# A state-space scan with a gated MLP: the rounding word of the weights is added on GpSimd from the fourth piece on

## The chip, the core and the metric

The kernel runs on one core of a Trainium2 chip. The metric is the device time of one execution in microseconds (us). The inputs lie in HBM, the output is written there.

## What is computed

Two stages. The first is a scan with decays, in chunks, over 4 batches x 8 heads x 768 tokens (head size 32, state size 16); the second is a gated MLP over the 3072 tokens of 256 channels, with 1536 hidden channels.

```python
la = log_a[:, :, sl]
cum = np.cumsum(la, axis=-1)
L = np.exp(cum[:, :, :, None] - cum[:, :, None, :]) * causal
M = np.einsum('bhin,bhjn->bhij', Cc, Bc) * L
y[:, :, sl] = np.einsum('bhij,bhjd->bhid', M, xc) + y_inter
...
state = decay_full[:, :, None, None] * state + np.sum(Bx, axis=2)
...
x = attn_out.transpose(0, 2, 1, 3).reshape(B * S, H * D)
g = x @ w_gate
silu = g * (1.0 / (1.0 + np.exp(-g)))
out = (silu * (x @ w_val)) @ w_out
```

The three weight matrices come as 64-bit floats. The kernel makes 32-bit floats of them itself.

## The kernel before

**Tiling.** The 768 tokens are cut into 6 blocks k of 128; a block with its 4 batches is a tile of 512 columns. Each block goes through the scan (tiles L, E, bc, xb, Cz, S, st, T, y), then through the MLP's gate and value products gv for the 12 pieces f of the hidden channels, the product sg of gate and value, the split of sg into a high part hh and a low part hl, and the projection po, whose result is drained to ob and stored. The last two blocks are multiplied as a pair with fewer products (px, py, pz, pr).

**Weights.** There are 18 pieces: wg0 to wg11 for gate and value, wo0 to wo5 for the projection. A piece i is fetched as 128 x 512 pairs of 32-bit words (tile wg3r, say: the low words `lw` are every second word, the high words `hw` the others). ScalarE makes the magnitude from the high word (`w_magnitude`, tile wg3w), VectorE bounds it (`w_range`), ScalarE makes the sign and exponent part (`w_sign`) and either engine the rest of the low word, scaled to one word (`w_rest`). VectorE shifts and joins them (`w_shift`, SCALAR_TENSOR_TENSOR in the trace), and `w_round` adds the rest as an integer. In the trace of before that addition is the row CUSTOM_DVE_ANT_0, in the order listings it is ISA. Block 0 multiplies pieces 0 to 8 with these 32-bit floats directly (gv<-xf,wg3w); pieces 9 to 11, the projection's pieces and all later blocks use a high part (wg3h, `w_high`) and a low part (wg3l, `w_low`).

**Buffers.** A raw piece lies in one of eight places until it is rounded; the fetch of a later piece into the same place waits for that (`uses=[("raw", i)]` in the plan). The fetches stand in SP's queue with the loads of bc, xb, L and E.

**What sets the order.** A planner (`Plan`) knows every step with its engine, its cost on that engine, its rank and the steps that it needs. It fills each engine's queue in turn, and what it finds is issued as it stands; each engine then works through its queue in that order. A step that may run on two engines goes where the planner's times favour it, so a changed cost or engine of one step moves others too. The rank of the rounding and what it needs stand in line 865:

```python
add("DVE", 0.6, do(w_round, i), r - 3.3 if i else -0.94,
    [("shift", i), ("rest", i), *([] if i else [("ce", 0)])], uses=[("raw", i)], gives=("round", i))
```

In the listings below sg_3_474<-gv_3_1_470 is the product of piece 3 (470 and 474 are buffer numbers), L<-L,dj a scan of the decays, L<-S,L a mix of decays with scores, T a state step.

Of the kernel before, what the change touches and what calls it, by code (L numbers as in the profile page):

```python
# [15 lines left out]
ALU = mybir.AluOpType  # L16
# [27 lines left out]
class Plan:  # L44
# [25 lines left out]
    def add(self, engine, cost, run, rank, needs=(), takes=(), uses=(), gives=None, kind=None, lag=0.0, rows=1.0, slack=0.0):  # L70
        engines = [(engine, cost)] if cost is not None else engine
        self.ops.append(Op(engines, run, rank, needs, takes, uses, gives, kind, lag, rows, slack))
# [137 lines left out]
def scan_moe_kernel(ctx: ExitStack, tc, rows, decays, bc, xb, wgv, wo, cst, out):  # L210
    nc = tc.nc
    PSUM = bass.MemoryType.PSUM
    te, ve, se, ge, sp = (
        Ordered(tc, e) for e in (nc.tensor, nc.vector, nc.scalar, nc.gpsimd, nc.sync)
    )

    def pool(name, bufs, stack=ctx, **kw):
        return stack.enter_context(tc.tile_pool(name=name, bufs=bufs, **kw))
# [5 lines left out]
    raw = pool("raw", RAW)  # L224
# [314 lines left out]
    def raw_home(i):  # L539
        if RAW <= i < RAW + MIXED:  # L540
            return mixed, "ws", "ws"
        if i == RAW + MIXED:
            return mixed, "mix", "mix"
        return raw, "wraw", "raw"
# [5 lines left out]
    part = [dict() for _ in pieces]  # L550
# [40 lines left out]

    def w_round(i):
        w = part[i]["w"]
        ve.tensor_tensor(out=w, in0=w, in1=part[i]["lw"], op=ALU.add)

    def w_high(i, e):
        hi = part[i]["hi"] = wts.tile([P, 4 * P], F32R, name=f"{pieces[i][4]}h")
# [133 lines left out]
    def gate_val(k, f, m):  # L731
        t = hid.setdefault((k, f), {})["gv"[m]] = ps_mm.tile([P, T], F32, tag="mm", name=f"gv{k}_{f}_{m}")
        if not k and f < WHOLE:
            w = part[f]["w"].bitcast(F32).rearrange("p (a b c) -> p a b c", b=2, c=P)
# [57 lines left out]
    rest = {}  # L792
# [20 lines left out]
    def do(f, *a):  # L813
        return lambda *e: f(*a, *e)
# [6 lines left out]
    add = plan.add  # L821
# [3 lines left out]
    for k in range(NB):  # L825
        begin[k] = t
        if k == PAIR:
            begin[k + 1], begin_sum[k], begin_sum[k + 1] = t, t + PAIR_LAG, t + NF * (GVP + PO)
            break
        t += (NF * GV if k else WHOLE * PACE0 + (NF - WHOLE) * GV) + ATT  # L830
        for i in (() if not k else (0, 1) if k == 1 else (k,)):
# [3 lines left out]
    def due(k, f=0):  # L835

        return begin[k] + f * (GV if k else PACE0) - (0 if k else max(f - WHOLE, 0) * (PACE0 - GV))

    def due_sum(k, f):
        return begin_sum[k] + f * (PO if k != PAIR else GVP + PO)  # L840
# [15 lines left out]
    for i in range(NW):  # L856
        r = due(0, i) - 1.0 if i < NF else due_sum(0, 2 * (i - NF)) - 1.0
        add("SP", 0.48, do(w_fetch, i), r - 9.0, [HELD[i]] if i in HELD else [] if not i else [("E", 0)] if i < HASTE else [("asked", 1)], takes=[(raw_home(i)[2], ("raw", i))], gives=("raw", i), lag=1.75 if i >= RAW + MIXED else 3.3 if not i else 1.4)
        plan.marked[plan.ops[-1]] = ("sent", i)
        add("Act", 0.565, do(w_magnitude, i), r - 5.5, [("raw", i)] + ([("xf", 2 * K - 1)] if i else []) + ([("rest", 1)] if i in (2, 3) else []), takes=[("sg" if i < NF else "w", ("w", i))], gives=("mag", i))  # L860
        add("DVE", 0.335, do(w_range, i), r - 4.5 if i else -1.05, [("mag", i)] + ([("round", 0), *([("round", 1)] if i == 2 else [])] if i > 1 else []), gives=("range", i))
        add([("Act", 0.57), ("DVE", 0.335)][: 1 + (i > 2)], None, do(w_rest, i), r - 4.5, [("mag", i), ("sign", i)], gives=("rest", i))
        add("Act", 0.57, do(w_sign, i), r - 5.4, [("mag", i)], gives=("sign", i))
        add("DVE", 0.6, do(w_shift, i), r - 4.2 if i else -1.05, [("range", i), ("sign", i)], gives=("shift", i))
        add("DVE", 0.6, do(w_round, i), r - 3.3 if i else -0.94, [("shift", i), ("rest", i), *([] if i else [("ce", 0)])], uses=[("raw", i)], gives=("round", i))
        early = WHOLE <= i < NF
        if i < NF and not early:
            r = due(1, i) - LATER
        later = [("M", 1, NP - 1)] if i < WHOLE else []
        add([("Act", 0.525), ("DVE", 0.34)], None, do(w_high, i), r - 2.7, [("round", i), *later], gives=("wh", i))  # L870
        whole_done = [("gv", 0, i, m) for m in range(2)] if i < WHOLE else []
        add("DVE", 0.6, do(w_low, i), r - 1.5, [("wh", i), *whole_done], uses=[("w", i)], gives=("wl", i))
# [7 lines left out]
    for k in range(NB):  # L880
        r = due(k)
# [3 lines left out]
        add("-", 0.0, do(new_decays, k) if k else lambda: None, z - 12, [("decays", k - 1)] if k else [], takes=[("L", L), ("E", E)], gives=("decays", k))  # L885
        late = [("raw", LATE[k])] if k in LATE else []

# [13 lines left out]
        if not k:  # L901
# [3 lines left out]
            for b in range(BATCH + 1):  # L905
                for i in range(2 if b < BATCH else 1):
                    t = ("spread", b, i)
                    last_one = int(i and b == BATCH - 1)
                    r = z + (3.0 if b == BATCH else 0.1 * b + i * (0.15 if b == BATCH - 1 else 0.5))
# [37 lines left out]
        uses = [L, E, XB, BC, *y, TT]  # L947
# [36 lines left out]
    r = due(PAIR) - 8.0  # L984
# [18 lines left out]
    for f in range(NF):  # L1003
        r = due(PAIR, f)
        slot = ("raw" if in_raw(f) else "ws", ("ws", f))
        for n, cost in enumerate((0.6, 0.2, 0.335, 0.2)):
            need = [("ws", f, n - 1)] if n else [("wl", f), MIXED_AFTER, *([("ws", f - 1)] if f else [])]
            gives = ("ws", f, n) if n < 3 else ("ws", f)
# [9 lines left out]
        w = [("wl", f), ("wh", f)]  # L1018
# [22 lines left out]
    for k in range(NB):  # L1041
        xs = [(t, k, i) for t in ("xh", "xl") for i in range(2 * K)]
        for f in range(NF):
            r = due(k, f)
# [15 lines left out]
            r = due_sum(k, f) - 4  # L1060
# [4 lines left out]
        for n, (m, t, fs) in enumerate(sums_of(k)):  # L1065
# [4 lines left out]
            r = due_sum(k, fs[0]) + n * 0.01  # L1070
# [22 lines left out]


WHOLE = 9
LATE = {2: NF + 2}
GATE, HASTE = dict(bc=0, aj=0, xb=0, an=1), 7
HELD = {1: ("M", 0, 0), 2: ("M", 0, 1), 3: ("M", 0, 3)}
# [52 lines left out]
```

## Time and profile before

| | |
|---|---|
| Median of 3 runs | 345.58 us |
| Lowest and highest | 344.18 and 346.75 us |
| Span of the profiled execution | 341.9 us |
| Median less that span | 3.7 us |
| TensorE busy | 337.3 us |
| VectorE busy | 256.8 us |
| ScalarE busy | 173.4 us |
| GpSimd busy | 4.1 us |

The profiled execution's own time is its span, from the first to the last instruction; the times of the runs also hold what lies around it. TensorE's matmuls are pipelined and their ends are modelled; start times are what to read there. A busy time counts an instruction from its start to its end; since the next may start a little before, what one costs in a full queue is the time from start to start.

### The profile page before, as it was taken

Reading aid. Unit: us, or ns where it says so; the run is one execution under the profiler, and the core shown is the slowest. Engines: PE = TensorE matmul, PEld = TensorE weight load, DVE = VectorE, ACT = ScalarE, POOL = GpSimd, SP = SyncE. Lnnn points to the kernel's source line nnn. Section 1 sums busy time; section 2 is a strip of 40 time slices with the busy share of each in tenths; the row PEclk is TensorE's granted clock in tenths of the full one; section 3 lists DMA queues with packets and bytes.
Section 4 is the critical chain, followed back from the end, with each engine's and each line's share of the span. In section 5 each row is a group of like instructions: output and inputs, shape, how many; then the busy total and the mean of one; then the engine's idle time right before and its main releaser. Section 6 shows DMA issues by size and latency. Waiting matters only on the chain.

```text
span 341.9 us, 7521 instructions
## 1 busy us (share of the span) xinstructions
PE 337.3 (99%) x3165; PEld 260.7 (76%) x3165; DVE 256.8 (75%) x473; ACT 173.4 (51%) x315; POOL 4.1 (1%) x11
## 2 busy tenths in 40 slices
PE   8999999999999999999999999999999999999996
PEld 7544457888777888877788778877788888888895
DVE  6999999979697586553599943595869999856540
ACT  3696897372684552421344432323656556444542
POOL 1300000000000000000000000000000000000000
PEclk9999999999999999999999999999999999999999
DMA  7789535950000931000380107500010000000101
GB/s 257 259 263 334 176 120 173 220 172 1 0 2 15 254 108 62 0 2 2 124 191 0 63 2 206 105 2 2 3 63 0 0 3 0 0 0 2 51 11 63
DMA packets 10602, 28.29 MB, mean 83 GB/s; under 512 B 1096, under 2 KB 2120, under 8 KB 10568
## 3 DMA queue, kind: packets, MB, share of 16 engines
q1 hardware_dynamic: 10152, 27.57, 27.3%
q8 instruction: 25, 0.41, 0.5%
q10 hardware_dynamic: 416, 0.23, 0.2%
q14 instruction: 9, 0.07, 0.1%
HBM read 24.46 MB, written 3.35 MB: 81 GB/s over the span
## 4 chain that ended last, share of the span: by engine, by line
PE 89%; DMA 5%; ACT 4%; SPq 0%; issue 0%; ACTq 0%
PE gv L199 34%; PE po L199 30%; PE py L199 7%; PE y L199 5%; PE px L199 5%; DMA wg9r<-in_wgv 4%; PE pr L199 2%; PE pz L199 2%; PE S L199 2%; DMA bc<-in_bc 1%; PE st L199 1%; PE rest L199 1%; ACT sg L199 1%; ACT Cz L199 0%; ACT wg9r L199 0%; ACT wg2r L199 0%
## 5 line engine op out<-in xcount | busy, mean ns | idle before, releaser
L199 ACT CAST hh<-sg 128x512 fp32r<-128x512 f32 x70 | 43.4, 621 | 51.2 <-PE po L199 29.0
L199 DVE TENSOR_TENSOR hl<-sg,hh 128x512 fp32r<-128x512 f32 x72 | 49.3, 689 | 25.8 <-ACT hh L199 25.5
L199 ACT ACTIVATE sg<-gv 128x512 f32<-128x512 f32 x48 | 28.5, 595 | 50.6 <-PE gv L199 50.4
L199 DVE TENSOR_TENSOR sg<-gv,sg 128x512 f32<-128x512 f32 x48 | 32.8, 686 | 27.1 <-PE gv L199 27.0
L199 DVE TENSOR_TENSOR_SCAN L<-L,dj 128x520 f32<-128x520 f32 x20 | 23.9, 1227 | 0.0
L199 DVE TENSOR_TENSOR L<-S,L 128x512 f32<-128x512 f32 x24 | 15.0, 683 | 0.4 <-PE S L199 0.4
L199 PE MATMUL py<-xht,ws 128*128 128x512 f32 x48 | 14.8, 389 | 0.0
L199 ACT COPY ob<-po 128x512 f32<-128x512 f32 (+1 forms) x12 | 6.6, 551 | 13.1 <-PE po L199 12.5
L199 ACT ACTIVATE sg<-px 128x512 f32<-128x512 f32 x12 | 7.2, 598 | 10.9 <-PE px L199 10.9
L199 ACT ACTIVATE Cz<-bc,cs 128x512 f32<-128x512 f32 x12 | 8.0, 714 | 8.5 <-DMA bc<-in_bc 8.5
L199 DVE TENSOR_TENSOR mix<-mix 128x128 f32<-128x128 f32 (+1 forms) x36 | 11.9, 330 | 0.2
L199 DVE TENSOR_TENSOR ps<-py,ps 128x512 f32<-128x512 f32 x12 | 8.2, 686 | 4.8 <-PE py L199 4.8
L199 PEld LDWEIGHTS y<-L,xb 64*32 64x32 f32 x768 | 7.3, 105 | 5.0 <-issue 2.8
L199 PE MATMUL y<-L,xb 64*32 64x64 f32 x768 | 10.9, 222 | 0.0
L199 PEld LDWEIGHTS py<-xht,ws 128*128 128x128 f32 x48 | 9.0, 188 | 1.9
L199 PE MATMUL po<-hh,wo0h 128*128 128x512 f32 (+1 forms) x26 | 10.3, 394 | 0.0
L199 PE MATMUL po<-hh,wo2h 128*128 128x512 f32 (+1 forms) x26 | 9.9, 382 | 0.0
L199 PE MATMUL po<-hh,wo3h 128*128 128x512 f32 (+1 forms) x26 | 9.9, 381 | 0.0
L199 PE MATMUL y<-bc,T 32*64 32x64 f32 x352 | 9.9, 228 | 0.0
L199 PE MATMUL po<-hh,wo5h 128*128 128x512 f32 (+1 forms) x26 | 9.8, 378 | 0.0
L199 PE MATMUL po<-hh,wo4h 128*128 128x512 f32 (+1 forms) x26 | 9.8, 378 | 0.0
L199 PE MATMUL po<-hl,wo0h 128*128 128x512 f32 (+1 forms) x26 | 9.7, 375 | 0.0
(485 smaller groups left out, 875.0 us busy)
## 6 DMA issues: line engine op xcount, KB each, us to landing
L<-clipped SPq DMA_DIRECT2D x10, 520.0 KB, 9.7
xb<-in_xb SPq DMA_DIRECT2D x6, 768.0 KB, 5.1
bc<-in_bc SPq DMA_DIRECT2D x6, 512.0 KB, 9.2
out<-ob SPq DMA_DIRECT2D x11, 256.0 KB, 2.1
E<-clipped SPq DMA_DIRECT2D x5, 260.0 KB
wg0r<-in_wgv SPq DMA_DIRECT2D x1, 512.0 KB, 7.4
wg1r<-in_wgv SPq DMA_DIRECT2D x1, 512.0 KB
wg2r<-in_wgv SPq DMA_DIRECT2D x1, 512.0 KB, 4.2
```

The costliest lines, as they stand in the source:

```text
L199: ins = getattr(self.engine, name)(*a, **k)
```

## The change

The integer addition of `w_round` is issued to GpSimd for pieces 3 to 17 (wg3 to wg11 and wo0 to wo5); pieces 0 to 2 stay on VectorE. The planner is told so, with another cost for the step.

```diff
--- before.py
+++ after.py
@@ -591,7 +591,7 @@
 
     def w_round(i):
         w = part[i]["w"]
-        ve.tensor_tensor(out=w, in0=w, in1=part[i]["lw"], op=ALU.add)
+        (ve if i < ROUND else ge).tensor_tensor(out=w, in0=w, in1=part[i]["lw"], op=ALU.add)
 
     def w_high(i, e):
         hi = part[i]["hi"] = wts.tile([P, 4 * P], F32R, name=f"{pieces[i][4]}h")
@@ -862,7 +862,7 @@
         add([("Act", 0.57), ("DVE", 0.335)][: 1 + (i > 2)], None, do(w_rest, i), r - 4.5, [("mag", i), ("sign", i)], gives=("rest", i))
         add("Act", 0.57, do(w_sign, i), r - 5.4, [("mag", i)], gives=("sign", i))
         add("DVE", 0.6, do(w_shift, i), r - 4.2 if i else -1.05, [("range", i), ("sign", i)], gives=("shift", i))
-        add("DVE", 0.6, do(w_round, i), r - 3.3 if i else -0.94, [("shift", i), ("rest", i), *([] if i else [("ce", 0)])], uses=[("raw", i)], gives=("round", i))
+        add(*(("DVE", 0.6) if i < ROUND else ("Pool", 1.45)), do(w_round, i), r - 3.3 if i else -0.94, [("shift", i), ("rest", i), *([] if i else [("ce", 0)])], uses=[("raw", i)], gives=("round", i))
         early = WHOLE <= i < NF
         if i < NF and not early:
             r = due(1, i) - LATER
@@ -1093,6 +1093,7 @@
 
 
 WHOLE = 9
+ROUND = 3
 LATE = {2: NF + 2}
 GATE, HASTE = dict(bc=0, aj=0, xb=0, an=1), 7
 HELD = {1: ("M", 0, 0), 2: ("M", 0, 1), 3: ("M", 0, 3)}
```

TensorE's and SP's instructions stand in the same order in both programs. GpSimd's queue ended with the clip of the decays (all). Before:

```order
L199 AFFINE_SELECT rows<-const-float32-1.0 128x512
L199 AFFINE_SELECT cs<-const-float32-1.0 128x128
L199 TENSOR_TENSOR xb_98<-xb_98,L_94 128x128 x4
L199 TENSOR_SCALAR all<-all 128x6x64
L1146 UNCONDITIONAL_BRANCH
```

Now, in the same place, the first of the fifteen additions follow:

```order
L199 TENSOR_TENSOR xb_98<-xb_98,L_94 128x128 x4
L199 TENSOR_SCALAR all<-all 128x6x64
L199 TENSOR_TENSOR wg3w<-wg3w,wg3r 128x512
L199 TENSOR_TENSOR wg4w<-wg4w,wg4r 128x512
L199 TENSOR_TENSOR wg5w<-wg5w,wg5r 128x512
L199 TENSOR_TENSOR wg6w<-wg6w,wg6r 128x512
```

The other eleven stand behind them in the order of the pieces.

VectorE's queue from the product of piece 1 to the first scan of L of block 1, before:

```order
L199 TENSOR_TENSOR sg_1_427<-gv_1_1_422,sg_1_427 128x512
L199 ISA wg3w<-wg3r,wg3w 128x1024
L199 TENSOR_SCALAR wg4w<-wg4w 128x512
L199 TENSOR_SCALAR wg5w<-wg5w 128x512
L199 SCALAR_TENSOR_TENSOR wg4w<-wg4w,wg4r 128x512
L199 SCALAR_TENSOR_TENSOR wg5w<-wg5w,wg5r 128x512
L199 ISA wg4w<-wg4r,wg4w 128x1024
L199 TENSOR_TENSOR sg_2_455<-gv_2_1_449,sg_2_455 128x512
L199 ISA wg5w<-wg5r,wg5w 128x1024
L199 TENSOR_SCALAR wg6w<-wg6w 128x512
L199 SCALAR_TENSOR_TENSOR wg6w<-wg6w,wg6r 128x512
L199 SCALAR_TENSOR_TENSOR L_367<-L_367,dj 128x520
```

And now:

```order
L199 TENSOR_TENSOR sg_1_427<-gv_1_1_422,sg_1_427 128x512
L199 TENSOR_SCALAR wg4w<-wg4w 128x512
L199 TENSOR_SCALAR wg4r<-wg4r 128x512
L199 SCALAR_TENSOR_TENSOR wg4w<-wg4w,wg4r 128x512
L199 TENSOR_SCALAR wg5w<-wg5w 128x512
L199 TENSOR_SCALAR wg5r<-wg5r 128x512
L199 SCALAR_TENSOR_TENSOR wg5w<-wg5w,wg5r 128x512
L199 TENSOR_SCALAR wg6w<-wg6w 128x512
L199 TENSOR_TENSOR sg_2_457<-gv_2_1_454,sg_2_457 128x512
L199 SCALAR_TENSOR_TENSOR wg6w<-wg6w,wg6r 128x512
L199 TENSOR_SCALAR Cz_478<-bc_389,cs 128x4x128 x2
L199 SCALAR_TENSOR_TENSOR L_367<-L_367,dj 128x520
```

The additions (ISA) are gone, two scalings of the rest word (wg4r, wg5r) and the two halves of Cz have come in, the latter ahead of the first scan of L.

VectorE's queue around the mixes of block 1, before:

```order
L199 TENSOR_SCALAR wg9w<-wg9w 128x512
L199 SCALAR_TENSOR_TENSOR T_106<-T_106,E_368 128x64 x4
L199 TENSOR_TENSOR L_367<-S_0_588,L_367 128x4x2x64
L199 TENSOR_TENSOR L_367<-S_1_589,L_367 128x4x2x64
L199 TENSOR_TENSOR L_367<-S_2_590,L_367 128x4x2x64
L199 SCALAR_TENSOR_TENSOR wg9w<-wg9w,wg9r 128x512
L199 TENSOR_TENSOR L_367<-S_3_591,L_367 128x4x2x64
L199 TENSOR_TENSOR sg_7_624<-gv_7_1_633,sg_7_624 128x512
L199 ISA wg9w<-wg9r,wg9w 128x1024
L199 TENSOR_SCALAR wg10w<-wg10w 128x512
L199 CAST wg9h<-wg9w 128x512
L199 SCALAR_TENSOR_TENSOR wg10w<-wg10w,wg10r 128x512
```

And now:

```order
L199 SCALAR_TENSOR_TENSOR wg9w<-wg9w,wg9r 128x512
L199 TENSOR_SCALAR wg10w<-wg10w 128x512
L199 SCALAR_TENSOR_TENSOR T_106<-T_105,E_368,T_106 128x64 x4
L199 SCALAR_TENSOR_TENSOR wg10w<-wg10w,wg10r 128x512
L199 SCALAR_TENSOR_TENSOR T_106<-T_106,E_368 128x64 x4
L199 TENSOR_TENSOR L_367<-S_0_592,L_367 128x4x2x64
L199 TENSOR_TENSOR L_367<-S_1_593,L_367 128x4x2x64
L199 TENSOR_TENSOR L_367<-S_2_594,L_367 128x4x2x64
L199 TENSOR_TENSOR L_367<-S_3_595,L_367 128x4x2x64
L199 TENSOR_TENSOR sg_7_628<-gv_7_1_640,sg_7_628 128x512
L199 TENSOR_TENSOR wg9l<-wg9w,wg9h 128x512
L199 TENSOR_SCALAR wg11w<-wg11w 128x512
```

Piece 9's shift and piece 10's shift stand ahead of the mixes, and the cast wg9h has gone to ScalarE's queue. Further on, the subtractions wg4l to wg8l stand ahead of block 1's xl instead of behind it, and the cast wg11h stands on VectorE.

## Rows read from the trace of the kernel before

**Rows 1.** The page: busy us, share and instructions of each engine.

```profile
PE 337.3 (99%) x3165; PEld 260.7 (76%) x3165; DVE 256.8 (75%) x473; ACT 173.4 (51%) x315; POOL 4.1 (1%) x11
```

**Rows 2.** Busy time by stretch: engines' busy us (x), PEclk, DMA share, GB/s.

```profile
0.00:23.20 23.20, 21.71 (x355) 13.51 (x356) 19.77 (x43) 14.48 (x27) 4.15 (x11) 1.00 0.76 264
23.20:61.10 37.90, 37.81 (x412) 21.16 (x411) 37.34 (x72) 31.04 (x60) 0.00 (x0) 1.00 0.65 207
61.10:338.80 277.70, 277.70 (x2401) 226.07 (x2399) 199.74 (x360) 127.51 (x229) 0.00 (x0) 1.00 0.19 51
338.80:341.90 3.10, 0.04 (x1) 0.00 (x0) 0.00 (x0) 0.37 (x1) 0.00 (x0) 1.00 0.22 74
```

**Rows 3.** VectorE's timeline: start us, us, engine, line, operation (21 to 31 us).

```profile
21.21 0.68 DVE L199 SCALAR_TENSOR_TENSOR wg3w<-wg3w,wg3r 128x512 int32<-128x512 int32 x1
...
23.23 0.68 DVE L199 CUSTOM_DVE_ANT_0 wg3w<-wg3r,wg3w 128x1024 uint16<-128x1024 uint16 x1
23.83 0.42 DVE L199 TENSOR_SCALAR wg4w<-wg4w 128x512 f32<-128x512 f32 x1
24.16 0.42 DVE L199 TENSOR_SCALAR wg5w<-wg5w 128x512 f32<-128x512 f32 x1
...
28.90 1.24 DVE L199 TENSOR_TENSOR_SCAN L<-L,dj 128x520 f32<-128x520 f32 x1
30.05 0.67 DVE L199 TENSOR_TENSOR sg<-gv,sg 128x512 f32<-128x512 f32 x1
```

**Rows 4.** GpSimd's timeline, the whole span.

```profile
0.88 0.66 POOL L199 TENSOR_SCALAR_AFFINE_SELECT rows<-const-float32-1.0 128x512 f32<-128x512 f32 x1 [0.39 <-POOLq L1140]
...
8.95 1.52 POOL L199 TENSOR_TENSOR xb<-xb,L 128x128 f32<-128x128 f32 x4 [7.13 <-DVE L L199]
10.66 1.49 POOL L199 TENSOR_SCALAR all<-all 128x384 f32<-128x384 f32 x1 [0.19 <-DMA all<-in_decays]
```

**Rows 5.** VectorE's timeline, 38 to 59 us.

```profile
38.35 0.29 DVE L199 TENSOR_TENSOR xb<-xb,L 128x128 f32<-128x128 f32 x1
38.55 0.42 DVE L199 TENSOR_SCALAR wg8w<-wg8w 128x512 f32<-128x512 f32 x1
...
41.22 0.68 DVE L199 CUSTOM_DVE_ANT_0 wg8w<-wg8r,wg8w 128x1024 uint16<-128x1024 uint16 x1
...
42.47 0.87 DVE L199 SCALAR_TENSOR_TENSOR T<-T,E,T 128x64 f32<-128x64 f32 x4
...
46.77 0.69 DVE L199 TENSOR_TENSOR L<-S,L 128x512 f32<-128x512 f32 x1
...
49.84 0.70 DVE L199 TENSOR_TENSOR wg9l<-wg9w,wg9h 128x512 fp32r<-128x512 f32 x1
...
57.39 1.43 DVE L199 TENSOR_TENSOR xl<-y,xh 128x256 fp32r<-128x256 f32 x4
```

**Rows 6.** ScalarE's timeline, the first load of bc after block 0.

```profile
29.64 1.33 ACT L199 ACTIVATE Cz<-bc,cs 128x512 f32<-128x512 f32 x2 [1.34 <-DMA bc<-in_bc]
```

**Rows 7.** TensorE's weight loads: what it loads, and when (25 to 62 us).

```profile
25.36 0.19 PEld L199 LDWEIGHTS gv<-xf,wg3w 128*128 128x128 f32 x1 [0.24 <-issue]
...
28.79 0.19 PEld L199 LDWEIGHTS gv<-xf,wg4w 128*128 128x128 f32 x1 [0.24 <-issue]
...
39.61 0.70 PEld L199 LDWEIGHTS st<-xb 64*32 64x32 f32 x64 [0.76 <-issue]
...
49.44 0.29 PEld L199 LDWEIGHTS y<-L,xb 64*32 64x32 f32 x32 [0.76 <-DVE wg9h L199]
...
51.33 0.42 PEld L199 LDWEIGHTS gv<-xh,wg9l 128*128 128x128 f32 x2
...
61.75 0.41 PEld L199 LDWEIGHTS gv<-xl,wg0h 128*128 128x128 f32 x2
```

**Rows 8.** The projection's last piece: VectorE's and TensorE's timelines.

```profile
106.10 0.69 DVE L199 TENSOR_TENSOR wo5l<-wo5w,wo5h 128x512 fp32r<-128x512 f32 x1 [0.69 <-ACT wo5h L199]
...
113.72 0.39 PE L199 MATMUL po<-hh,wo5l 128*128 128x512 f32 x1
```

## The prediction

> **What bounds the kernel now.** I read the page's busy line first. TensorE is busy 337.3 of 341.9 us, no other engine more than 76% [rows 1]. The next view is the busy time by stretch, because a share of 99% leaves open where the last per cent lies [rows 2]. It lies outside the reach of this change: 1.49 us of TensorE idle time before 23.2 us (23.20 less 21.71), 3.06 us at the very end, where only the last drain and the last store are left, and between them 0.09 us from 23.2 to 61.1 and nothing at all from 61.1 to 338.8. The granted clock is 1.00 in every stretch. So TensorE's own instruction stream is the time, and another engine matters only where it makes that stream wait. VectorE is the engine that comes nearest to that: from 23.2 to 61.1 it is busy 37.34 of 37.90 us, and there the weights are rounded that block 0 multiplies by.
>
> TensorE's instructions stand in the same order before and after; the change reorders only VectorE, ScalarE and GpSimd. That leaves little to win: the most that can be gained is those 0.09 us. What has to be worked out is whether anything TensorE waits for now comes too late.
>
> **What is removed.** Fifteen additions leave VectorE. One takes 0.68 us, and the next instruction starts 0.60 us after it [rows 3]; that start-to-start time is what one costs in a full queue. Nine of them (pieces 3 to 11) stood in the full stretch, 9 x 0.60 = 5.4 us; six (the projection's pieces) stood behind it.
>
> **What is added on GpSimd.** Fifteen additions of 128x512 words. The trace has none of that shape, so I bound one by its neighbours on that engine [rows 4]. From below: a 128x512 select, which reads only a constant, took 0.66 us. From above: the clip of 128x384 took 1.49 us with one input and two operations, and by elements 512 columns would be 1.49 x 512/384 = 1.99 us. Nearest is the row of four two-input products of 128x128, 1.52 us for the same 512 columns in all. I take 1.5 us, and keep 0.66 and 1.99.
>
> **What is moved, walked through.** The scheduler refills VectorE: it takes over the rest words of pieces 4 and 5, both halves of Cz of block 1 and the cast wg11h from ScalarE, gives the cast wg9h to ScalarE, and pulls five low-part subtractions ahead of block 1's xl. I walk the new order from 23.23 us, where the two orders part, with the start-to-start times of the old trace: 0.60 us for a 128x512 instruction with two inputs, 0.33 for one with a single input (24.16 - 23.83), 1.15 for a scan (30.05 - 28.90) [rows 3], 0.20 for an xb product (38.55 - 38.35), 0.87 for a group of four state steps, 1.43 for the four parts of xl [rows 5].
>
> First leg, to Cz: five single-input instructions and four with two, 1.65 + 2.40 us, end at 27.28. There VectorE stops. Cz needs bc, and in the old trace ScalarE could start it only at 29.64, with bc's transfer as its releaser [rows 6]. Behind the waiting Cz stand the first scan of L, the product sg_3 and the xb products. So VectorE now loses 2.36 us here in which it used to work on other things; what the removed additions gave back so far (three, 1.8 us) is eaten by this wait, and the first scan starts at 30.30, not at 28.90. Who waits for that next is TensorE's state sums st.
>
> Second leg, from 29.64 to the last xb product: four single-input instructions (1.32, the two halves of Cz among them), four scans (4.60), four with two inputs (2.40), four xb (0.80), 9.12 us in all: 38.76 instead of 38.55. TensorE loads st at 39.61 [rows 7]. Slack 0.85 us, 1.06 before: no new wait.
>
> Third leg, to the last mix of L: five with two inputs (3.00), one scan (1.15), two with one (0.66), two groups of state steps (1.74), four mixes (2.40): 47.71. TensorE loads y at 49.44 [rows 7]; the old mix was through at 46.77 + 0.60 = 47.37 [rows 5]. Slack 1.73 us, 2.07 before. Then sg_7 and wg9l: 48.91, with 51.33 as the time TensorE loads it [rows 7]: 2.42 us of slack where the old order (49.84 + 0.60 = 50.44) had 0.89.
>
> Fourth leg, to xl: fourteen with two inputs (8.40), three with one (0.99), the four parts of xl (1.43): 59.73, against the load at 61.75 [rows 7]. Slack 2.02 us; the old xl was through at 57.39 + 1.43 = 58.82, so 2.93 before. VectorE gives 0.9 us of slack away here and gets it on wg9l.
>
> The rounded words themselves: piece 3's shift ends at 21.21 + 0.68 = 21.89 [rows 3], so GpSimd is through at 23.4 and TensorE loads it at 25.36 [rows 7]. Each further piece has 3.43 us on TensorE (28.79 - 25.36), more than twice the 1.5 us of an addition. Piece 8: shifted at 39.36 in the walk, rounded at 40.9; the old rounding ended at 41.22 + 0.68 = 41.90 [rows 5]. In SP's queue the fetches of wg11 and wo0 to wo5 wait for the rounding that frees their buffer, and the loads of block 2 stand behind wo3; these all come earlier or at the same time, so the queue is not held up. The casts wg9h and wg10h now wait on ScalarE for GpSimd with sg_8 behind them, but their words are rounded by 44.2 and 46.0, and the walk wants the two casts at 48.3 and 49.2 and sg_8 at 50.4. Of the projection's pieces the last is ready at 106.79 and loaded at 113.72 [rows 8], 6.9 us of cover; an addition that is 0.9 us longer doesn't use it up.
>
> The sum: 5.4 us and more taken off VectorE, none of it on the path; the waits that bound TensorE all keep 0.85 us or more. 341.9 + 0.0, at most 0.1 less. The profiled span stands 3.7 us under the median of the runs (345.58), and the change touches nothing outside the span: **345.6 us**, no change. If the cover at st is used up, each further us of lateness on VectorE costs one us.
>
> **The rivals.** (1) **VectorE and GpSimd get in each other's way.** GpSimd is idle from 23.2 us on [rows 2], so no row of this trace shows a two-input GpSimd instruction beside a full VectorE. If each addition stops VectorE for its whole 1.5 us: one (piece 7) stands ahead of st, 1.5 - 0.85 = 0.65 us late; three (7 to 9) ahead of y, 4.5 - 1.73 = 2.8 late; five (7 to 11) ahead of xl, 7.5 - 2.02 = 5.5 late. Pieces 3 to 6 fall ahead of the wait for bc, which absorbs them. These are one lateness, not three to be added: 5.5 us, 351.1. If half of it falls beside instructions that read PSUM (the four mixes and the products sg) and is not felt, 3.75 - 2.02 = 1.7 us, 347.3. I put this rival at the y figure, 348.4; it is slower than before, and it decides from a loss of 2.02 / 5 = 0.40 us per addition. The Trainium skill, in SBUF — State Buffer, section "Who interferes with whom", says that a VectorE instruction with two SBUF inputs and a GpSimd instruction that reads SBUF use the same port, and that the second to start is blocked until the first is through; most of the walk is of that kind. By that rule the loss is real, and this rival would be the forecast; no run here shows it yet.
>
> (2) **The addition is far slower than its neighbours**, since it is on 32-bit integers with every second word of one operand. It decides from about 3.4 us: piece 3 then misses 25.36, and every piece takes longer than TensorE's 3.43. At 4.5 us four in a row from 21.89 end at 39.9, where piece 6 is wanted at 25.36 + 3 x 3.43 = 35.65: 4.2 us, 349.8. Against it stand the rows above, all under 2 us.
>
> (3) **Faster**, by more than the 0.1 us of idle time that stands behind 23.2 us: only if TensorE's own instructions ran faster without VectorE's extra traffic. Nothing in the rows speaks for it; 342 or less.
>
> **How the numbers follow.** A difference under 1% (3.46 us) is about what a measurement of this kernel can't tell from none; the three runs alone span 344.18 to 346.75. Forecast, no new wait: 0.60. Rival 1: 0.30, of which 0.09 past 349.0. Rival 2: 0.05. Rival 3: 0.03, and 0.02 for a slowdown that I don't see. So faster 0.03, same 0.60 + 0.21 + 0.01 (a mild rival 2) = 0.82, slower 0.15. The range goes from 343.9, the low end of the runs seen, to 349.2, which takes in rival 1 at its y figure and leaves out its worst case and most of rival 2.
>
> **What would show it.** Right: TensorE's idle time from 23.2 to 61.1 stays near 0.09 us; GpSimd's fifteen rows have a mean between 0.66 and 1.99 us; VectorE stands idle for some 2.4 us before Cz with bc as releaser; wg9l is through well ahead of 50.44. Wrong, for rival 1: VectorE's start-to-start times grow past 0.60 us (1.15 for a scan) beside a GpSimd row, and TensorE waits for xb, L or xl. Wrong, for rival 2: TensorE waits for a piece wg3w to wg8w with GpSimd as releaser.

## The result, and the profile after

The changed kernel takes 349.81 us (median of 4 runs, 349.44 to 350.42), the kernel before 345.50 beside it (4 runs): slower by 4.3 us. The ratio given for the runs is 1.0146, with a 95% interval from 1.0113 to 1.0178, or 5.0 us (0.0146 x 345.5); it isn't the quotient of the two medians, which is 1.0125. The profiled execution has a span of 348.6 us instead of 341.9. These 6.7 us are more than the runs show: a run's time stands 1.67 to 2.42 us above its own span wherever both are known, so 341.9 is a short execution of the kernel before, and 348.6 is the longest of the changed kernel's four.

The page's busy line answers to [rows 1], the busy time by stretch to [rows 2].

```profile
PE 340.0 (98%) x3162; PEld 262.7 (75%) x3165; DVE 260.3 (75%) x465; ACT 169.2 (49%) x308; POOL 28.1 (8%) x26
```

```profile
23.20:61.10 37.90, 34.03 (x296) 17.33 (x295) 37.87 (x62) 26.70 (x50) 15.49 (x9) 0.95 0.63 192
61.10:100.00 38.90, 38.90 (x261) 31.89 (x261) 33.12 (x55) 20.18 (x37) 5.55 (x4) 1.00 0.37 100
100.00:338.80 238.80, 238.80 (x2216) 193.49 (x2215) 169.31 (x311) 107.05 (x195) 2.85 (x2) 1.00 0.17 46
```

VectorE has 8 instructions fewer and is busy 3.5 us longer, which already says that some of its instructions now take longer. In the stretch from 23.2 to 61.1 TensorE is busy 34.03 us where it was 37.81, with a granted clock of 0.95. Behind 61.1 it never stands idle: all of the loss lies ahead of that.

TensorE's waits name who was late (engine, what waited, for whom: us in total, times, longest).

```profile
PE y L199 <- DVE L L199: 2.2, 4, 1.3
PE st L199 <- DVE xb L199: 1.7, 1, 1.7
```

TensorE's timeline has them in their places. Its rows after:

```profile
42.88 0.35 PE L199 MATMUL st<-xb 64*32 64x64 f32 x16 [1.66 <-DVE xb L199]
43.16 1.98 PE L199 MATMUL gv<-xf,wg7w 128*128 128x512 f32 x4
45.07 1.21 PE L199 MATMUL S<-Cz,bc 32*64 32x128 f32 x64
...
52.97 0.30 PE L199 MATMUL y<-L,xb 64*32 64x64 f32 x2 [1.35 <-DVE L L199]
...
56.97 1.22 PE L199 MATMUL gv<-xh,wg9h 128*128 128x512 f32 x2
```

and the same places in the kernel before:

```profile
40.40 1.98 PE L199 MATMUL gv<-xf,wg7w 128*128 128x512 f32 x4
42.31 1.85 PE L199 MATMUL S<-Cz,bc 32*64 32x128 f32 x64
...
50.99 0.73 PE L199 MATMUL gv<-xh,wg9h 128*128 128x512 f32 x2
```

Piece 7's first product is 2.76 us later (43.16 less 40.40), of which 1.66 is the wait for xb; 0.87 was there from block 0's first product on (15.97 instead of 15.10), a start that varies among the kernels profiled here (15.08 to 16.23, and 15.31 in experiment 4, whose queues are in the changed kernel's order) and isn't the change's. Piece 9's first product is 5.98 us later (56.97 less 50.99), and from 59.08 on everything is 6.6 us later, to the end.

The last stretch of that, from the first row of y to the second pair of products with wg9h, runs at a lower clock. The busy time by stretch, same columns as above:

```profile
51.50:56.97 5.47, 3.26 (x98) 2.10 (x97) 5.47 (x11) 4.90 (x10) 0.54 (x1) 0.81 0.41 130
56.97:59.08 2.11, 2.11 (x11) 1.72 (x7) 2.11 (x3) 2.00 (x4) 1.30 (x1) 0.68 0.00 0
```

The granted clock is 0.81 and 0.68 where it was 1.00 [rows 2]: part of these stretches passed at 1.2 GHz instead of 2.4. By single microseconds it is 0.50, the lower level, from 55 to 58. It follows the row of waits of TensorE for the mixes and is back at 1.00 from 59.08. The two products with wg9h took 1.22 us there, 0.73 before. The clock is not the root, though: one of the four executions had a mean clock of 1.000 (the other three 0.995), and its span was still 347.8 us, no shorter than the shortest of the other three (347.7). Nor is a lower clock the change's alone: of 63 executions of the kernel before, timed beside the experiments, 4 have a mean clock of 0.995 or less.

Now the engines that were late. GpSimd's timeline, the additions of pieces 3 to 10, where the kernel before had nothing [rows 4]:

```profile
23.61 1.41 POOL L199 TENSOR_TENSOR wg3w<-wg3w,wg3r 128x512 int32<-128x512 int32 x1 [11.13 <-DVE wg3w L199]
27.27 2.68 POOL L199 TENSOR_TENSOR wg4w<-wg4w,wg4r 128x512 int32<-128x512 int32 x1 [2.24 <-DVE wg4w L199]
29.91 1.73 POOL L199 TENSOR_TENSOR wg5w<-wg5w,wg5r 128x512 int32<-128x512 int32 x1
31.60 1.48 POOL L199 TENSOR_TENSOR wg6w<-wg6w,wg6r 128x512 int32<-128x512 int32 x1
39.63 2.12 POOL L199 TENSOR_TENSOR wg7w<-wg7w,wg7r 128x512 int32<-128x512 int32 x1 [6.55 <-DVE wg7w L199]
43.56 2.10 POOL L199 TENSOR_TENSOR wg8w<-wg8w,wg8r 128x512 int32<-128x512 int32 x1 [1.82 <-DVE wg8w L199]
47.89 1.34 POOL L199 TENSOR_TENSOR wg9w<-wg9w,wg9r 128x512 int32<-128x512 int32 x1 [2.22 <-DVE wg9w L199]
50.64 1.40 POOL L199 TENSOR_TENSOR wg10w<-wg10w,wg10r 128x512 int32<-128x512 int32 x1 [1.41 <-DVE wg10w L199]
```

VectorE's timeline, the rows that lie beside them, in answer to [rows 3, 5]:

```profile
23.40 1.92 DVE L199 SCALAR_TENSOR_TENSOR T<-T,E 128x64 f32<-128x64 f32 x4
...
29.31 1.18 DVE L199 SCALAR_TENSOR_TENSOR wg6w<-wg6w,wg6r 128x512 int32<-128x512 int32 x1
30.53 2.83 DVE L199 TENSOR_SCALAR Cz<-bc,cs 128x512 f32<-128x512 f32 x2
33.28 1.23 DVE L199 TENSOR_TENSOR_SCAN L<-L,dj 128x520 f32<-128x520 f32 x1
...
39.42 1.23 DVE L199 TENSOR_TENSOR_SCAN L<-L,dj 128x520 f32<-128x520 f32 x1
40.57 1.46 DVE L199 TENSOR_SCALAR wg8w<-wg8w 128x512 f32<-128x512 f32 x1
...
44.51 1.45 DVE L199 TENSOR_SCALAR wg9w<-wg9w 128x512 f32<-128x512 f32 x1
...
48.02 1.89 DVE L199 SCALAR_TENSOR_TENSOR T<-T,E,T 128x64 f32<-128x64 f32 x4
...
50.43 1.89 DVE L199 SCALAR_TENSOR_TENSOR T<-T,E 128x64 f32<-128x64 f32 x4
52.24 2.47 DVE L199 TENSOR_TENSOR L<-S,L 128x512 f32<-128x512 f32 x4
```

Beside an addition a scaling takes 1.46 us instead of 0.42, a group of four state steps 1.89 instead of 0.87, and the two halves of Cz 2.83. The four mixes, with no addition beside them, keep their 0.60 us from start to start (2.47 for four that overlap a little). Two of the additions are themselves long, 2.12 and 2.10 us: they begin while a scan is under way (39.63 against a scan that runs from 39.42 to 40.65, and 43.56 against one from 43.35 to 44.58).

### The profile page after: what moved, and what is told of

The parts are those of the page before. It is cut to its first block, busy times and chain, and to the rows that moved or that the text cites. A ratio compares the mean times of both kernels' runs of the same rounds, so it can differ in the third digit from the quotient of the medians.

```text
span 348.6 us, 7534 instructions
## 1 busy us (share of the span) xinstructions
PE 340.0 (98%) x3162; PEld 262.7 (75%) x3165; DVE 260.3 (75%) x465; ACT 169.2 (49%) x308; POOL 28.1 (8%) x26
## 4 chain that ended last, share of the span: by engine, by line
PE 83%; DVE 4%; issue 1%; ACT 0%; DVEq 0%; ACTq 0%
PE gv L199 31%; PE po L199 29%; PE py L199 7%; PE px L199 5%; PE y L199 5%; PE pr L199 2%; PE pz L199 2%; PE S L199 1%; DVE T L199 1%; DVE L L199 1%; PE st L199 1%; DVE wg8w L199 1%; DVE sg L199 0%; DVE E L199 0%; DVE wg9w L199 0%
## 5 line engine op out<-in xcount | busy, mean ns | idle before, releaser
L199 ACT CAST hh<-sg 128x512 fp32r<-128x512 f32 x69 | 42.6, 621 | 50.8 <-PE po L199 27.9
L199 DVE TENSOR_TENSOR_SCAN L<-L,dj 128x520 f32<-128x520 f32 x20 | 25.0, 1281 | 0.0
L199 PE MATMUL y<-L,xb 64*32 64x64 f32 x768 | 12.0, 226 | 2.2 <-DVE L L199 2.2
L199 ACT ACTIVATE Cz<-bc,cs 128x512 f32<-128x512 f32 x10 | 6.7, 718 | 7.6 <-DMA bc<-in_bc 7.6
```

Source lines behind the costliest of these rows:

```text
L199: ins = getattr(self.engine, name)(*a, **k)
```

## The experiments

Two theories stood at first. **Blocking** (theory A in the expectations): while GpSimd adds, VectorE's instructions wait, and the order matters only by what the addition meets. **Order** (rival B): the refilled VectorE queue is too late by itself, whichever engine adds. The expectations name a rival C as well: GpSimd rounds the words too late for TensorE. Later kernels ask what in the addition does the blocking (its reading, its writing or its length), and what the walk of the prediction had wrong. The changed kernel is called after here. Each is timed against the kernel before, on the same chip. In experiments 1, 4, 9 and 10 every queue stands in after's order, in 2, 3, 5, 6 and 7 in that of before; 8 changes after's behind the additions that it holds back.

**1. The order without the engine.** The planner's table of after, but the addition is issued to VectorE at the place where GpSimd's would be issued.

```diff
-        (ve if i < ROUND else ge).tensor_tensor(out=w, in0=w, in1=part[i]["lw"], op=ALU.add)
+        ve.tensor_tensor(out=w, in0=w, in1=part[i]["lw"], op=ALU.add)
```

> The queues stand in the changed kernel's order, but every rounding is back on VectorE. Theory A (a GpSimd addition stops VectorE, about 1.0 us each by the changed kernel's rows): GpSimd is idle from 23 us on, so 1.000 to 1.004 of the time before; five roundings at 0.60 us make xl at most 3.0 - 2.02 = 1 us late. Rival B (the new order does it, Cz waiting on VectorE for bc first of all): still 1.011 to 1.017. Rival C (the rounded words come later from GpSimd, and TensorE waits for them): 1.000 to 1.003.

Measured: 1.0070 (1.0046 to 1.0094), 346.36 us. That meets none of the three ranges; it is about half of the loss. In its trace the mixes end at 50.54 us, where they ended at 47.37 before [rows 5]: the additions of pieces 9 and 10, and the scaling and shift of piece 10, now stand ahead of them in VectorE's own queue. So the order has a price of its own when VectorE also does the adding; this kernel doesn't tell what the order costs when it does not (experiment 4 does).

**2. The engine without the order.** The queues of before, with the addition of pieces 3 to 17 issued to GpSimd.

```diff
-        ve.tensor_tensor(out=w, in0=w, in1=part[i]["lw"], op=ALU.add)
+        (ve if i < 3 else ge).tensor_tensor(out=w, in0=w, in1=part[i]["lw"], op=ALU.add)
```

> The queues stand in the order of before, and the roundings of pieces 3 to 17 are issued to GpSimd. Theory A: seven roundings stand ahead of wg9l, each takes 0.60 us from VectorE's queue and gives back about 1.0 to 1.1: 7 x 0.45 less the old slack of 0.89 is 2.3 us, and some 1 to 2 us of TensorE at the lower clock behind its wait: 1.006 to 1.013; the rows show single-input and state-step instructions of VectorE at two to four times their old length beside GpSimd. Rival B: 1.000. Rival C: 1.000 to 1.004, and TensorE waits with GpSimd's wg words as releasers.

Measured: 1.0004 (0.9986 to 1.0022), 344.49 us, under theory A's range and as rival B had it. One of GpSimd's additions, and then VectorE's rows beside it and beside piece 3's, both timelines:

```profile
47.07 1.29 POOL L199 TENSOR_TENSOR wg9w<-wg9w,wg9r 128x512 int32<-128x512 int32 x1 [4.98 <-DVE wg9w L199]
```

```profile
22.06 1.91 DVE L199 SCALAR_TENSOR_TENSOR T<-T,E 128x64 f32<-128x64 f32 x4
...
46.86 0.68 DVE L199 TENSOR_TENSOR L<-S,L 128x512 f32<-128x512 f32 x1
47.46 0.68 DVE L199 TENSOR_TENSOR sg<-gv,sg 128x512 f32<-128x512 f32 x1
48.06 0.59 DVE L199 TENSOR_SCALAR wg10w<-wg10w 128x512 f32<-128x512 f32 x1
```

The addition of piece 9 runs from 47.07 to 48.36. The mix and the product sg that run in that time, both of which read one input from PSUM, take their usual 0.68; the scaling behind them waits out the last 0.3 us. Blocking is there in this kernel too (T 1.91, and a product bc 1.45 instead of 0.68 beside piece 8's addition). The stretches of its eight additions 3 to 10 add up to 4.83 us (1.04 on T, 0.51 and 0.92 on piece 6's scaling and shift, 0.45 and 0.46 on two products xb, 0.77 on bc, 0.17 and 0.51 on the scalings of pieces 10 and 11). Leaving VectorE gave, by the start-to-start time, 8 x 0.60 = 4.80. The two cancel. Six of the eight lie ahead of the last mix (4.15 taken, 3.60 given), and it starts at 46.86 where it started at 46.77 [rows 5]; the rest went into short idle times of VectorE that the kernel before had on the way. TensorE waits for VectorE nowhere from 23 us on.

So neither half alone makes the whole loss, the engine none that can be told here and the order 1.0070 with VectorE adding: it is what the additions meet in the new order.

**3. The projection's pieces alone.** As 2, with `i < 12` for `i < 3`.

> The order of before; only the six roundings of the projection's pieces are issued to GpSimd. Theory A: VectorE is blocked there too, but it has idle time between 61 and 107 us and 6.9 us of cover for the last piece: 1.000 (0.998 to 1.002). Rivals B and C: 1.000 as well. It tells whether an addition on GpSimd costs anything where VectorE's queue isn't full.

Measured: 0.9995 (0.9969 to 1.0021), 344.10 us. The six additions behind 61 us cost and bring nothing that can be told, which goes with after's TensorE standing idle nowhere behind 61.1. The profiled execution is one of the longer ones (347.70 us, mean clock 0.995), and its trace has a lower clock without any addition on GpSimd: ahead of 61 us GpSimd adds nothing here. TensorE's timeline, and the busy time of a stretch behind that row:

```profile
44.95 2.03 PE L199 MATMUL S<-Cz,bc 32*64 32x128 f32 x60 [1.50 <-ACT T L199]
```

```profile
47.00:49.00 2.00, 2.00 (x3) 0.97 (x4) 2.00 (x4) 1.93 (x5) 0.00 (x0) 0.50 0.00 0
```

Here it was ScalarE that was late, by 1.50 us at the scores S, and the granted clock behind it is 0.50 too.

**4. The new order with no addition at all.** After, but the rounding word of pieces 3 to 17 is left out, on either engine.

```diff
-        (ve if i < ROUND else ge).tensor_tensor(out=w, in0=w, in1=part[i]["lw"], op=ALU.add)
+        if i < ROUND:
+            ve.tensor_tensor(out=w, in0=w, in1=part[i]["lw"], op=ALU.add)
```

> The changed kernel's queues, with the addition left out for pieces 3 to 17: their rounding word is never added, and GpSimd is idle from 23 us on. It is the prediction's walk as it stood, with nothing that could block VectorE. Theory A: no new wait for TensorE, 1.000 (0.998 to 1.002), the last mix of L through about 1.7 us ahead of y. Rival B (the new order by itself has a cost that the walk misses, Cz's wait for bc for one): 1.004 to 1.007, as with all roundings back on VectorE.

Measured: 0.9998 (0.9971 to 1.0024), 344.63 us, and TensorE waits for nothing of VectorE's from 23 us on (once for ScalarE, 0.5 us at S). This is the prediction's walk with its assumption made true. VectorE's timeline:

```profile
30.21 0.88 DVE L199 TENSOR_SCALAR Cz<-bc,cs 128x512 f32<-128x512 f32 x2 [2.48 <-DMA bc<-in_bc]
31.00 1.23 DVE L199 TENSOR_TENSOR_SCAN L<-L,dj 128x520 f32<-128x520 f32 x1
...
38.29 0.40 DVE L199 TENSOR_SCALAR wg8w<-wg8w 128x512 f32<-128x512 f32 x1
...
45.79 2.47 DVE L199 TENSOR_TENSOR L<-S,L 128x512 f32<-128x512 f32 x4
```

Set beside after, whose queues have the same order, this is the clean measure of the blocking. After's mixes start at 52.24, 6.45 us later than 45.79. Of that 2.28 is there at the first scan (33.28 less 31.00; 1.95 of it is the longer Cz, 0.32 its later start), and the other 4.17 are four stretches of 1.03 to 1.06 us, one for each addition from piece 7 to 10: the scalings wg8w and wg9w and the two groups of state steps (0.86 us here). Set beside experiment 1, it gives the price of an addition in VectorE's own queue: its mixes are through at 48.19 instead of 50.54, and four additions (pieces 7 to 10) lie between, 0.59 us each.

**5. An addition that nobody needs.** Before, with an extra addition on GpSimd behind each rounding, whose result is not used. The copy and the fill below take its place in two more kernels; a copy reads one word for each that it writes, a fill reads nothing.

```diff
         ve.tensor_tensor(out=w, in0=w, in1=part[i]["lw"], op=ALU.add)
+        if i >= 3:
+            ge.tensor_tensor(out=part[i]["lw"], in0=w, in1=part[i]["lw"], op=ALU.add)
```

> The kernel before as it is, rounding on VectorE, and behind each rounding from piece 3 on GpSimd adds the rounded word to the raw low word, which nobody reads any more. No engine waits for the result; only the raw piece's buffer comes free later. Theory A: VectorE keeps its 0.60 us per rounding and loses about 1.0 on top: six such additions stand ahead of wg9l, 6 x 1.0 - 0.89 = 5.1 us, and 1 to 2 us at the lower clock: 1.015 to 1.022. Rival B: 1.000. Rival C: 1.000, since no word comes later.

Measured: 1.0223 (1.0199 to 1.0247), 351.98 us, just past the upper end of theory A's range. GpSimd's and VectorE's timelines, at piece 8:

```profile
46.21 1.62 POOL L199 TENSOR_TENSOR wg8r<-wg8w,wg8r 128x512 int32<-128x512 int32 x1 [1.89 <-ACT wg11w L199]
```

```profile
46.60 1.89 DVE L199 SCALAR_TENSOR_TENSOR T<-T,E,T 128x64 f32<-128x64 f32 x4
```

Nothing is reordered here, nothing that TensorE needs comes from GpSimd, VectorE still does its own roundings, and the kernel is 7.4 us slower. From 23 to 62 us TensorE waits 4.6 us, all of it for VectorE (xb, L and the words wg9h, wg9l and wg10l). The raw buffers come free later as well, but so they do with the fill of experiment 7, by less, and that costs nothing. That shows blocking by itself.

**6. A copy** (`ge.tensor_copy(part[i]["lw"], w)`), in the same place.

> The kernel before, and behind each rounding from piece 3 on GpSimd copies the rounded word over the raw low word that nobody reads any more: one input from SBUF instead of two. Theory A, by now in this form: while a GpSimd instruction that reads SBUF runs, a VectorE instruction with its operands in SBUF waits, and one that reads PSUM doesn't. A copy then costs about its own length less what falls beside PSUM readers, as the idle addition did (0.93 us each of 1.3 to 1.5): 1.008 to 1.020. Rival D (it is the second operand: two streams of GpSimd on one port): under 1.003.

Measured: 1.0037 (1.0014 to 1.0060), 345.22 us, between the two ranges. The same two timelines in the same place:

```profile
43.30 1.05 POOL L199 COPY wg8r<-wg8w 128x512 int32<-128x512 int32 x1 [1.85 <-DVE wg8w L199]
```

```profile
43.71 1.25 DVE L199 SCALAR_TENSOR_TENSOR T<-T,E,T 128x64 f32<-128x64 f32 x4
```

The copy takes 0.67 us where nothing is in its way, the addition 1.30, and the stretches are shorter (the state steps 1.25 us, 1.89 beside the idle addition). So a second word read by GpSimd isn't needed for blocking, as rival D had it: one is enough, and it lasts less long.

**7. A fill** (`ge.memset(part[i]["lw"], 0)`), in the same place.

> The same place, but GpSimd only fills the raw low word with zeros: it reads nothing and writes as much. Theory A with the read side as the shared thing: two-input VectorE instructions keep their 0.60 us, and only single-input ones from SBUF to SBUF (casts, scalings), if any, are stretched: 1.000 to 1.004. Rival E (any GpSimd access stops VectorE, or GpSimd's activity as such): 1.008 or more, with stretched scans and subtractions.

Measured: 1.0004 (0.9977 to 1.0030), 344.09 us. GpSimd's fills, and VectorE's rows beside them:

```profile
41.10 0.56 POOL L199 MEMSET wg7r<- 128x512 int32 x1 [7.00 <-DVE wg7w L199]
44.97 0.58 POOL L199 MEMSET wg8r<- 128x512 int32 x1 [3.32 <-DVE wg8w L199]
```

```profile
41.10 0.83 DVE L199 TENSOR_SCALAR wg8w<-wg8w 128x512 f32<-128x512 f32 x1
...
44.79 0.68 DVE L199 TENSOR_TENSOR bc<-bc,E 128x512 f32<-128x512 f32 x1
45.39 0.86 DVE L199 SCALAR_TENSOR_TENSOR T<-T,E,T 128x64 f32<-128x64 f32 x4
```

The two-input rows bc and T run beside a fill at their old 0.68 and 0.86 us, though T for 0.16 us only; a subtraction wg2l that starts 0.29 us before the last fill of the nine ends (58.22 + 0.60 less 58.53) keeps its 0.68 as well. Nor does bc hold up the fill: 0.58 us, where the copy that met bc in the same place took 1.05. The scaling, with a single input, is stretched from 0.42 to 0.83. A two-input instruction of VectorE is thus in the way of what GpSimd reads; for a scaling, writing is enough (one row). The Trainium skill, in SBUF — State Buffer, section "Who interferes with whom", says the same: a VectorE instruction with two SBUF inputs is in the way of a GpSimd instruction that reads SBUF, not of one that only writes it; one with at most one SBUF input, outside the modes with two ports, is in the way of neither; and one in such a mode contends with GpSimd for the ports that they share. The rows agree at each of the three, if the scaling is in such a mode, which no row names; that it takes 0.33 us from start to start where two-input instructions take 0.60 [rows 3] goes with it.

**8. Two additions moved beside the mixes.** After, with the additions of pieces 9 and 10 held back until the second group of state steps is done, in the plan and by a dependency.

```diff
+        passed["step", k, q] = ins.ins.name
...
+        if i in (9, 10):
+            wait_for(ins, ("step", 1, K - 1))
```

> The changed kernel; the additions of pieces 9 and 10 wait for block 1's last state step, so that they run beside the four mixes, which read PSUM, and no longer beside the state steps. Theory A: two state-step groups get back 1.03 us each; 2.06 us less wait at y, of which some 0.7 may return as a wait for wg9l: 1.008 to 1.011. Rival B (the order alone makes it slow) and rival C (late words; the words now come even later): 1.014 or more.

Measured: 1.0079 (1.0058 to 1.0100), 347.11 us. VectorE's and GpSimd's timelines:

```profile
46.91 0.86 DVE L199 SCALAR_TENSOR_TENSOR T<-T,E,T 128x64 f32<-128x64 f32 x4
...
49.08 2.47 DVE L199 TENSOR_TENSOR L<-S,L 128x512 f32<-128x512 f32 x4
```

```profile
49.29 1.30 POOL L199 TENSOR_TENSOR wg9w<-wg9w,wg9r 128x512 int32<-128x512 int32 x1 [4.72 <-ACT wg11r L199]
50.53 1.30 POOL L199 TENSOR_TENSOR wg10w<-wg10w,wg10r 128x512 int32<-128x512 int32 x1
```

Two additions run for 2.54 us beside four mixes, and the mixes take 2.47 us as ever; the state steps are back at 0.86. The same fifteen additions on the same engine cost 0.67% less of the time (1.0146 less 1.0079, 2.3 us; 1.6 us by the quotients of the medians), about the two stretches of 1.03 us that are gone. The intervals of the two kernels don't meet. The mean clock of its profiled execution is 1.000, so some of the gain may be clock, and VectorE's and ScalarE's orders differ from after's behind the mixes (the cast wg10h is on VectorE here).

**9 and 10. Which additions.** After's order, with pieces 3 to 6 alone on GpSimd (the diff), and with pieces 7 to 11 alone (`7 <= i < NF` in its place); the rest on VectorE.

```diff
-        (ve if i < ROUND else ge).tensor_tensor(out=w, in0=w, in1=part[i]["lw"], op=ALU.add)
+        (ge if 3 <= i < 7 else ve).tensor_tensor(out=w, in0=w, in1=part[i]["lw"], op=ALU.add)
```

> The changed kernel's order; only pieces 3 to 6 are added on GpSimd, all later ones on VectorE. The prediction had it that these four fall ahead of the wait for bc, which absorbs them: then 1.004 to 1.007, as with all roundings on VectorE in this order. Theory A from the changed kernel's rows (Cz 2.83 us for two halves instead of 0.87, first scan about 2 us late): that lateness goes through to st and y, 1.010 to 1.014.

> The changed kernel's order; only pieces 7 to 11 are added on GpSimd, 3 to 6 and the projection's pieces on VectorE. Theory A: four roundings (2.4 us) leave VectorE's queue ahead of y, and four of its instructions are stretched by 1.03 us each (wg8w, wg9w and two groups of state steps): 1.7 us more than with all roundings on VectorE, 1.007 + 0.005 = 1.012. If the losses of the two groups of pieces simply add, 1.0146 - (1.0093 - 1.007) gives 1.012 as well. If pieces 3 to 6 alone make the changed kernel slow: 1.007 or less.

Measured: 1.0093 (1.0072 to 1.0115), 347.85 us, and 1.0122 (1.0075 to 1.0168), 348.74 us. They are to be set against experiment 1, which differs from each by those pieces alone: 0.0023 and 0.0052 more than its 1.0070. Neither is clear of the noise, since both intervals overlap that of experiment 1; that the sum, 0.0075, comes out beside after's 1.0146 less 1.0070 is closer than these intervals warrant. What each group does is read from the traces. TensorE's waits for VectorE's xb and L are 0.6 us in experiment 1 (L alone), 1.5 with pieces 3 to 6 on GpSimd (0.6 for xb, 0.9 for L), 2.0 with pieces 7 to 11 (L alone) and 3.9 in after. In the first kernel VectorE's timeline shows

```profile
30.90 2.10 DVE L199 TENSOR_SCALAR Cz<-bc,cs 128x512 f32<-128x512 f32 x2 [0.76 <-DMA bc<-in_bc]
```

VectorE does still wait for bc here, and then Cz takes 2.10 us instead of 0.88.

The 1.0093 lies above the range for pieces 3 to 6 absorbed and a little under theory A's; the 1.0122 is what was expected.

No version beats the kernel before: experiments 2, 3 and 4 equal it, as far as can be told, and there was little to win, with 0.09 us of TensorE idle time from 23.2 to 338.8 [rows 2] and up to 0.64 us at the scores S (see the next section).

## Why the prediction was wrong

**The step that failed** is this sentence of the walk: "I walk the new order from 23.23 us, where the two orders part, with the start-to-start times of the old trace". Those times were taken with GpSimd idle, and the change is what ends that: beside an addition a scaling took 1.46 us instead of 0.42, four state steps 1.89 instead of 0.87, and TensorE waited 3.87 us for xb and L, where the walk had it wait for neither. The prediction had the point as its first rival, with a price and a chance of 0.30, and put 0.60 on its not happening for want of a row. Experiment 5 shows that the rival is real, experiment 4 that nothing else in the walk was wrong by enough to matter.

**The gain**: at most 0.09 us, and 0.60 us for each addition that leaves VectorE. The second holds (0.59 by experiments 1 and 4), and experiment 2 shows it taken back. The first is too low a bound. At the scores S the kernel before takes 1.78 us from start to start (42.31 to 44.09), after 1.14 and experiment 2 1.13; a weight load there waits 0.33 us for ScalarE's T. In the busy times, which go by modelled ends, only 0.09 of that shows as idle. So up to 0.64 us could be had at S. The wait isn't the change's: with the queues of before it is gone in experiment 2 and 1.50 us in experiment 3, with those of after 0.53 in experiment 4.

**The base**: 345.6 took 3.7 us as what lies around the span. A run's time stands 1.67 to 2.42 us above its own span; the rest is that the profiled execution was a short one. The forecast of no change didn't depend on it.

**The addition's own time** was put at 1.5 us between 0.66 and 1.99. Undisturbed it is 1.30; the fifteen rows have a mean of 1.60 (15.56 us for pieces 3 to 11 and 8.40 for the six of the projection). Rival 2 didn't come in: TensorE waits for no rounded piece.

**The walk without blocking**, against experiment 4: the wait for bc 2.36 forecast, 2.48 measured; the first scan 30.30 and 31.00; the last mix through at 47.71 and 45.79 + 4 x 0.60 = 48.19; no new wait for VectorE, and none came. Its errors of 0.5 and 0.7 us are inside the slack of 0.85 to 2.4.

**"Pieces 3 to 6 fall ahead of the wait for bc, which absorbs them"** was wrong for half of them. Piece 3's addition stretched T by 1.05 us and piece 4's the shift of piece 6 by 0.50, ahead of the wait, and these are absorbed: Cz starts at 30.53, 0.32 later than in experiment 4, although the run was 0.87 behind at its start. But GpSimd's queue runs late as well. Piece 4's addition took 2.68 us, and those of pieces 5 and 6 ran from 29.91 to 33.08, on top of Cz, behind the wait: 2.83 us for the two halves where experiment 4 has 0.88, 1.95 lost.

**Rival 1's price**, 348.4, was too low; the measured 349.81 lies between it and its upper bound of 351.1. It had 1.5 us for each of three additions ahead of y. The runs show less for each and more of them: 1.03 to 1.06 from piece 7 on, with piece 10's addition ahead of the mixes as well, and 1.95 from pieces 5 and 6. It had half of them "beside instructions that read PSUM" as its mild case; in after's order none of the eight lies beside such an instruction alone. The threshold of 0.40 us per addition was passed (7.67 us of stretches for the eight, 0.96 each).

And one term was missing. In TensorE's timeline the 5.98 us at wg9h go so: 0.87 from the start; 1.66 of waiting at st and 0.23 around it; 0.58 given back by the end of piece 8, most of it at the scores S, as told under the gain; then 5.35 us from there (51.62, which is 52.97 less 1.35) to wg9h, where the kernel before has 1.55 (49.44 to 50.99). Of these 3.80 extra, 2.21 are the four waits for L. The rest, 1.59, are products issued in small groups between waits and products at half the clock, which the trace here doesn't separate; the second of the two stretches above adds another 0.62 behind wg9h (2.11 us, where before the same products went from 50.99 to 52.48). So about 2.2 us of this execution's loss come behind the waits, and the prediction charged a wait at one microsecond for one. The size of that term varies: the execution with a mean clock of 1.000 has a span only 0.8 us shorter than the profiled one.

**What was to show it**: "VectorE's start-to-start times grow past 0.60 us (1.15 for a scan) beside a GpSimd row, and TensorE waits for xb, L or xl". That is what the trace shows, for xb and L. Of the signs of being right only one came, GpSimd's mean of 1.60 us: VectorE doesn't stand idle before Cz, wg9l only starts at 55.23, and TensorE stands idle for 3.87 us in the stretch.

## What to carry to other kernels

Moving work to an idle engine isn't free because the engine is idle: first ask, in the new order, which instruction stands beside each moved one, and whether both read SBUF; here an addition of 1.30 us on GpSimd cost VectorE 0.96 us on average, more than the 0.60 it had saved. The same addition was free beside instructions that take an input from PSUM, so the place in the other engine's queue is worth more than the choice of engine. And when the trace of before can't show an interaction since one side of it was idle, an idle dummy instruction measures it in one run, before the real change is planned.

## What was not expected of the hardware

- **Who waits depends on who started.** A scan that is under way makes the addition late (2.12 and 2.10 us instead of 1.30) and loses nothing itself (1.23 us); an addition under way makes a scaling, a state step or Cz wait, a scaling or a group of state steps by 1.03 to 1.06 us where the two start close together (a little more in experiment 5, where a scaling goes from 0.42 to 1.52 and a subtraction from 0.68 to 1.79).
- **Single-input scalings are blocked as well** (0.42 to 1.46 us beside an addition, to 0.83 beside a fill), which the prediction, with its eye on two-input instructions, didn't name; its price of a whole addition covered them.
- **An input from PSUM is enough to be left alone**: four mixes 2.47 us and a product sg 0.68 us, with GpSimd adding all the while.
- **A wait of TensorE can cost more than its length**: in after the four waits at y, 2.21 us, were followed by granted clocks of 0.81 and 0.68, and in experiment 3 the 1.50 us at S by 0.50. It doesn't follow always: behind the 1.66 us at st the clock of after is 1.00 (43.16 to 51.50), and with the two additions beside the mixes, and with the idle addition (4.6 us of waits), the profiled executions show a mean clock of 1.000. What decides that is left open.
